# Loading the rows of w_out a pair ahead, and giving the product stage of w3 and w_out a written order on every engine

## The chip, the cores and the metric

One core of a Trainium2 chip. TensorE (PE) multiplies and loads weights, VectorE (DVE) and ScalarE (ACT) do the elementwise work, and SyncE (SP) and GpSimd (POOL) issue the DMAs here. The metric is the device time of one execution in microseconds (us). TensorE's clock has two levels, 1.2 and 2.4 GHz; the profile gives the granted clock as a share of the upper one.

## The reference

```python
scores = scale * q @ k.T - log(S)            # batch 8, 12 heads, S 448, head dim 64
attn = 1 / (1 + exp(-scores))
x = (attn @ v)  -> (3584, 768)               # tokens x model
a = x @ w1;  b = x @ w2                      # (768, 1024) each
h = a * b @ w3                               # (1024, 1024)
out = h @ w_out                              # (1024, 768)
```

The kernel takes the product of the last two matrices first: `w3 @ w_out`, 1024x768, and then `g = a * b` times that product. Every 2x2 block product is done in seven half-size products (Winograd's form), and every fp32 operand is split into a high and a low part (`high = round(x)`, `low = x - high`), so that one product becomes three matmuls: high*high, high*low, low*high.

## The kernel before

Four stages follow one another. In the first, attention runs in bursts, and beside it the weights are decoded. `up(g)` (L491) then forms `a * b` for four groups of tokens `g` and writes it to `g_dram`; the last group, `up(3)`, runs alone after the attention. It has 8 column blocks `fc` of 7 products `k` of 9 matmuls each (3 chunks `kc` by 3 parts), 63 matmuls to an `fc`. Its four banks in PSUM are `up0`, `up1` and two of `av`; product 2 goes on in the bank of product 0, 3 in that of 1, and 6 in that of 4, so product 2 may start only when ACT has copied product 0 out (`p`, L551).

While `up(3)` runs, `split_wo` (L746) prepares the operands made of `w_out`: for each of four `jc` it loads four rows from `wo_dram` (`load`, L748, on the GpSimd queue, into the pool `tw`, 7 buffers), and makes from them seven operands, each with a high part on ACT (`high_part`, L761) and a low part on DVE (`low_part`, L765). It is a generator, and one step of it follows every ten matmuls of `up(3)` (L791: a turn); between the loads of one `jc` and the first use lie two turns. At turns 40 and 41 the first two weights made of `w3` are split too (`split_w3`, L737).

Up to `order.close()` (L798) the instructions of all five engines stand in the order in which the program emits them (`manual_schedule(engines=ALL)`, L583). From L803 on only PE and SP do; for ACT, DVE and POOL the planner sets the order.

The product stage (L856 to L908) forms `w3 @ w_out`: four `ic` of seven products (counted here 0 to 27 as `n = ic * 7 + turn`, in the order of `PLAN`, L854) of 12 matmuls each. At the head of product `n` the program emits the split of the `w3` operand of product `n + 2` (`split_w3`: ACT high, DVE low, three buffers `w3s`) and the load of `n + 4` (`load_w3` on SP, two buffers `w3`, so that it waits for the low half of `n + 2`). The products of an `ic` take turns in two PSUM banks, `up` and `av` (two buffers each): turn 2 goes on in the bank that turn 0 filled, and must wait until ACT has copied turn 0 out (`p`, L881); turn 3 waits for the add of turn 1 (`u2`, L888), and so on. The results are summed and split into the seven stationary operands of the last stage (`put`, L850: high on ACT, low on DVE): A11 after turn 2, A22 after turn 4, A12 after turn 5, and S2, S3, S1, S4 after turn 6, where four sums are made first.

Then `phase_w` closes (L909), which frees the pool `p3`, and the last stage starts: product 0 has its moving block `b11` split already (in product 14 of the stage before), and the blocks `b12` and `b22` are loaded into the pool `p5`, which takes the place of `p3` (`load_block`, L820, on SP). `prepare_block(1)` splits `b21` into tiles of `p5`, too. Product 2 needs `t2 = b22 - b11`.

`combine` (L311) ends each pair of heads: ACT copies the attention result out of PSUM to `x`, and for the last quarter of the work DVE adds `x` to `s1` (L321).

Of the kernel before, what the change touches and what calls it, by code (L numbers as in the profile page):

```python
# [11 lines left out]
F32 = mybir.dt.float32  # L12
# [3 lines left out]
ALU = mybir.AluOpType  # L16
# [9 lines left out]
def sigmoid_attention_bilinear_ffn(  # L26
# [16 lines left out]
    nc = tc.nc  # L43
    B, H, D, S = qT.shape
    DM, DF = w1.shape[0], w1.shape[1] // 2
    NT = B * S
    P = 128
# [6 lines left out]
    NM = DM // 2  # L54
# [188 lines left out]
    def total(out, in0, in1, op):  # L243
        nc.vector.tensor_tensor(out=out, in0=in0, in1=in1, op=op)  # L244

    def second(g, kc):
        a11, s1 = xf.pop((g, "A11", kc)), xf[g, "A21", kc]
        total(a11, s1, a11, ALU.subtract)
        xf[g, "S2", kc] = a11
        split_operand(g, "S2", kc, a11)  # L250

    def third(g, kc):
        a22 = xf[g, "A22", kc]
        total(a22, a22, xf[g, "S2", kc], ALU.subtract)
        split_operand(g, "S3", kc, a22)

    def fourth(g, kc):
        a12 = xf.pop((g, "A12", kc))
        total(a12, a12, xf.pop((g, "S2", kc)), ALU.subtract)
        split_operand(g, "S4", kc, a12)  # L260
# [3 lines left out]
    class Units:  # L264

        def __init__(self, g):
            self.g = g
            names = ("A11", "S1", "S2") if g < NG - 1 else ("A11", "A12", "A22")
            self.left = [(name, kc) for kc in range(KH) for name in names]
            rest_of = ("A12", "A22", "S3", "S4") if g < NG - 1 else ("S2", "S3", "S1", "S4")  # L270
            self.left += [(name, kc) for name in rest_of for kc in range(KH)]
# [16 lines left out]
        def emit(self, unit):  # L288
            self.left.remove(unit)
            name, kc = unit  # L290
            if name == "S2":
                second(self.g, kc)
            elif name == "S3":
                third(self.g, kc)
            elif name == "S4":
                fourth(self.g, kc)
            else:
                split_operand(self.g, name, kc, xf[self.g, {"S1": "A21"}.get(name, name), kc])
# [12 lines left out]
    def combine(n, acc):  # L311

        b, hp = divmod(n, NPAIR)
        g, odd = divmod(b, 2)
        right, kc = divmod(hp, KH)
        name = (("A11", "A12"), ("A21", "A22"))[odd][right]
        x = xf[g, name, kc] = pf.tile([P, S], F32, name=f"{name}{kc}", bufs=1 if odd else 2)
        nc.scalar.copy(out=x, in_=acc[:, :S])
        if odd and right:
            s1 = xf[g, "A21", kc]  # L320
            total(s1, s1, x, ALU.add)  # L321

    def words(w, columns):
        return w.rearrange("(c p) (f u) -> p c f u", p=P, u=2)[:, :, columns]
# [98 lines left out]
    NH = NF // 2  # L423
    jobs = []
    for ic in range(NH):
        for i, j in ((0, 0), (0, 1), (1, 0), (1, 1)):
            src = words(w3T, slice((i * NH + ic) * P, (i * NH + ic + 1) * P))
            jobs.append((src[:, j * NH:(j + 1) * NH], None))
        for jc in (ic, ic + NH):
            for ms in (slice(0, NM), slice(NM, DM)):  # L430
                src = w_out[jc * P:(jc + 1) * P].rearrange("p (m u) -> p m u", u=2)[:, ms]
# [141 lines left out]
    def take(stream, n):  # L573
        done = 0
        for _ in itertools.islice(stream, n):
            done += 1
        return done

    ET = mybir.EngineType

    order = ExitStack()
    ALL = {ET.PE, ET.SP, ET.Activation, ET.DVE, ET.Pool}
# [143 lines left out]
    p3 = phase_w.enter_context(tc.tile_pool(name="p3", bufs=2, side="right"))  # L726
# [14 lines left out]
            w3s[n] = w  # L741

    def temp():
        return p3.tile([P, NM], F32, name="tw", bufs=7)

    def split_wo():  # L746

        def load(jc):  # L748
            rows = []
            for at in (jc, jc + NH):  # L750
                for ms in (slice(0, NM), slice(NM, DM)):
                    rows.append(temp())
                    nc.gpsimd.dma_start(out=rows[-1], in_=wo_dram[at, :, ms])
            return rows

        for jc in range(NH):
            b11, b12, b21, b22 = load(jc)
            for _ in range(2):
                yield

            def high_part(k, src):  # L761
                nc.scalar.copy(out=seven[k][0][:, jc], in_=src)
                return k, src

            def low_part(k, src):  # L765
                h, l = seven[k]
                nc.vector.tensor_tensor(out=l[:, jc], in0=src, in1=h[:, jc], op=ALU.subtract)

            last = high_part(0, b11)
            yield  # L770
            for k, src in ((1, b21), (6, b22)):
                following = high_part(k, src)
                low_part(*last)
                last = following
                yield
            t3, t2 = temp(), temp()
            for k, out, in0, in1 in (
                (3, t3, b22, b12), (4, b12, b12, b11), (2, t2, b22, b12), (5, b21, b21, t2)
            ):
                total(out, in0, in1, ALU.subtract)  # L780
                following = high_part(k, out)
                low_part(*last)
                last = following
                yield
            low_part(*last)

    pieces = split_wo()
    for n in range(2):
        load_w3(n, nc.gpsimd)
    turn = 0  # L790
    while take(filler, 10):  # L791
# [3 lines left out]
            load_w3(turn - 38, nc.gpsimd)  # L795
        turn += 1
    assert turn > 42 and not take(pieces, 1)
    order.close()  # L798
    phase_x.close()
    share_upper(None)  # L800
    phase_s.close()
    everything = ExitStack()
    everything.enter_context(tc.manual_schedule(engines={ET.PE, ET.SP}))  # L803

    ps = ctx.enter_context(tc.tile_pool(name="ps2", bufs=2, space=PSUM))
    pw = ctx.enter_context(tc.tile_pool(name="pw", bufs=4, side="left"))
    A11, A12, A22, S1, S2, S3, S4 = range(7)
# [5 lines left out]
    def stationary(which):  # L813
        return stat[which]
# [3 lines left out]
    own = {g: {} for g in range(NG)}  # L818
# [18 lines left out]
    def split_block(dst, src):  # L837
        for fs in HALVES:
            split(dst[0][:, fs], dst[1][:, fs], src[:, fs], nc.scalar.copy, nc.vector)
            yield  # L840
# [7 lines left out]
    ready_blocks = {}  # L848

    def put(which, ic, src):  # L850
        h, l = stationary(which)
        split(h[:, ic], l[:, ic], src, nc.scalar.copy, nc.vector)

    PLAN = {0: (0, True), 2: (1, True), 1: (0, False), 3: (1, False),  # L854
            4: (0, True), 5: (1, False), 6: (0, False)}
    for ic in range(NH):  # L856
        bank = {}
        for turn, (k, (which, start)) in enumerate(PLAN.items()):
            n = ic * 7 + turn
            split_w3(n + 2)  # L860
            load_w3(n + 4)
            if n in (7, 8):
                load_block(0, BLOCKS[n - 7])
            elif n == 14:
                ready_blocks[0] = moving(p4)
                for _ in split_block(ready_blocks[0], own[0]["b11"]):
                    pass
            if start:
                bank[which] = ps.tile([P, 512], F32, name="up", tag=("up", "av")[which], bufs=2)
            acc = bank[which][:, :NM]  # L870
            w = w3s.pop(n)
            th, tl = seven[k]
            for jc in range(NH):
                for m, (i, t) in enumerate(((0, th), (0, tl), (1, th))):
                    nc.tensor.matmul(  # L875
                        acc, w[:, i, jc], t[:, jc], start=start and jc == 0 and m == 0,
                        stop=jc == NH - 1 and m == 2, skip_group_check=True,
                    )
            if k == 0:
                p = temp()  # L880
                nc.scalar.copy(out=p, in_=acc)  # L881
            elif k == 1:
                c11 = temp()
                nc.scalar.copy(out=c11, in_=acc)
                put(A11, ic, acc)
            elif k == 2:
                u2 = temp()
                total(u2, acc, p, ALU.add)  # L888
            elif k == 3:
                u3 = temp()  # L890
                total(u3, acc, p, ALU.add)
            elif k == 4:
                total(u3, acc, u3, ALU.add)
                put(A22, ic, u3)
            elif k == 5:
                total(p, acc, p, ALU.add)
                put(A12, ic, p)
            else:
                total(u2, acc, u2, ALU.add)
                s3 = temp()  # L900
                total(s3, c11, u2, ALU.subtract)
                total(u2, u2, u3, ALU.add)
                total(c11, u2, c11, ALU.subtract)
                put(S2, ic, c11)
                put(S3, ic, s3)
                put(S1, ic, u2)
                total(p, p, c11, ALU.subtract)
                put(S4, ic, p)  # L908
    phase_w.close()  # L909
    p5 = ctx.enter_context(tc.tile_pool(name="p5", bufs=1, side="right"))  # L910
    for name in ("b12", "b22"):
# [65 lines left out]
    for n in range(7 * NG):  # L977
        which, bank, start = ORDER[n % 7]
# [3 lines left out]
        for mc in range(MC):  # L982
# [3 lines left out]
            acc = accs[bank, mc][:, :S]  # L986
# [38 lines left out]
```

## Time and profile before

| | us |
|---|---|
| median of 3 runs | 984.55 |
| the three runs | 983.85, 984.55, 986.32 |
| the profiled execution, its own time | 986.56 |
| its span, first to last instruction | 984.8 |
| `up(3)`, fc 1 to 7 | 607.11 to 706.90 |
| product stage of w3 and w_out | 707.98 to 773.25 |
| last stage | from 773.25 |

The trace is that of one execution, and its durations belong to it; it lies 2.0 us over the median of the runs. Times of the trace are counted from the span's start.

### The profile page before, as it was taken

The numbers are of one execution on the slowest core, as the hardware profiler recorded it, in microseconds if no ns is written. First come the engines' busy times: TensorE is split into PE (matmuls) and PEld (weight loads), VectorE is DVE, ScalarE is ACT, GpSimd is POOL, SyncE is SP. The second block draws the span as 40 slices with busy tenths as digits, with TensorE's granted clock in tenths as the row PEclk, the third lists the DMA queues.
The fourth block names the chain that finished last, engine by engine and source line by source line (L and its number), as shares of the span: only waits on it lengthen the run. The fifth ranks groups of instructions, "written<-read, shape, count | busy, mean of one in ns | idle before, by whom it ended". The sixth has DMA issues, their size and how long they took to land.

```text
span 984.8 us, 14267 instructions
## 1 busy us (share of the span) xinstructions
PE 959.2 (97%) x5190; PEld 750.4 (76%) x5190; DVE 700.3 (71%) x1154; ACT 413.5 (42%) x620; POOL 115.8 (12%) x204
## 2 busy tenths in 40 slices
PE   8999999999999999999999998799999999999998
PEld 4444666667665999849999556798889989999997
DVE  5869878987558877798868966456568777474643
ACT  6887556655556111281112660223145433223230
POOL 1110222232100121200211201211100000000000
PEclk9999999999999999999999999899999999999999
DMA  8764577776565899968999825788553334342402
GB/s 264 247 209 136 196 248 259 238 264 215 199 208 179 284 403 338 354 206 287 330 397 335 277 63 167 248 274 282 161 174 110 123 103 141 113 150 103 159 29 84
DMA packets 97605, 210.66 MB, mean 214 GB/s; under 512 B 10496, under 2 KB 57600, under 8 KB 97536
## 3 DMA queue, kind: packets, MB, share of 16 engines
q1 hardware_dynamic: 80880, 145.55, 45.0%
q0 software_dynamic: 16512, 63.98, 18.3%
q8 instruction: 41, 0.67, 0.3%
q14 instruction: 28, 0.23, 0.1%
q10 hardware_dynamic: 144, 0.23, 0.1%
HBM read 151.52 MB, written 58.20 MB: 213 GB/s over the span
## 4 chain that ended last, share of the span: by engine, by line
PE 82%; DVE 8%; DMA 5%; issue 3%; ACT 1%; POOL 1%; SPq 0%; ACTq 0%; POOLq 0%; DVEq 0%
PE up L542 36%; PE up L990 20%; PE av L219 10%; PE sp L196 7%; PE up L875 4%; PE av L227 2%; PE third L196 1%; PE sp L206 1%; DMA tw<-wo_dram 1%; DMA w<-w_dram 1%; DVE A L244 1%; DVE lS L81 1%; DMA vv<-vL 1%; DMA g_dram<-c 1%; DMA gf_b<-g_dram 1%
## 5 line engine op out<-in xcount | busy, mean ns | idle before, releaser
L542 PE MATMUL up<-hS,w 128*128 128x448 f32 x702 | 218.6, 371 | 9.7 <-DVE c L512 6.6
L542 PE MATMUL up<-hA,w 128*128 128x448 f32 x522 | 164.2, 369 | 0.4 <-ACT a L178 0.3
L542 PEld LDWEIGHTS up<-hS,w 128*128 128x128 f32 x702 | 133.5, 190 | 27.7 <-DVE c L512 7.9
L178 ACT ACTIVATE a<-sp,bias 128x896 f32<-128x896 f32 x132 | 130.0, 1011 | 52.7 <-PE sp L196 27.2
L542 PE MATMUL up<-lS,w 128*128 128x448 f32 x351 | 129.9, 370 | 0.8 <-DVE lS L81 0.8
L990 PE MATMUL up<-gl,sh 128*128 128x448 f32 x336 | 123.3, 367 | 1.5 <-DVE gl L81 1.5
L219 PE MATMUL av<-a,vv 128*64 128x448 f32 x576 | 123.7, 551 | 0.5 <-DMA vv<-vL 0.5
L990 PE MATMUL up<-gh,sh 128*128 128x448 f32 x336 | 123.3, 367 | 0.0
L990 PE MATMUL up<-gh,sl 128*128 128x448 f32 x336 | 123.3, 367 | 0.0
L542 PEld LDWEIGHTS up<-hA,w 128*128 128x128 f32 x522 | 98.7, 189 | 14.0 <-issue 4.2
L542 PE MATMUL up<-lA,w 128*128 128x448 f32 x261 | 95.8, 367 | 0.0
L551 ACT COPY p<-up 128x448 f32<-128x448 f32 x32 | 17.1, 533 | 175.9 <-PE up L542 158.8
L219 PEld LDWEIGHTS av<-a,vv 128*64 128x64 f32 x576 | 35.1, 136 | 65.9 <-issue 64.8
L512 DVE TENSOR_TENSOR u<-up,p 128x448 f32<-128x448 f32 x64 | 39.9, 623 | 58.7 <-PE up L542 55.4
L542 PEld LDWEIGHTS up<-lS,w 128*128 128x128 f32 x351 | 66.8, 190 | 7.2 <-DVE lS L81 2.1
L990 PEld LDWEIGHTS up<-gl,sh 128*128 128x128 f32 x336 | 63.1, 188 | 7.4 <-DVE gl L81 1.8
L990 PEld LDWEIGHTS up<-gh,sh 128*128 128x128 f32 x336 | 63.1, 188 | 5.8 <-ACT p L959 0.2
L990 PEld LDWEIGHTS up<-gh,sl 128*128 128x128 f32 x336 | 63.1, 188 | 5.7
L875 PE MATMUL up<-th,w3s 128*128 128x384 f32 x224 | 59.5, 344 | 4.7 <-DVE tw L244 2.0
L512 DVE TENSOR_TENSOR u<-up,u 128x448 f32<-128x448 f32 x64 | 39.8, 621 | 28.1 <-PE up L542 27.6
L80 ACT CAST gh<-gf_b 128x896 fp32r<-128x896 f32 x40 | 35.8, 941 | 56.4 <-PE up L990 55.0
L81 DVE TENSOR_TENSOR gl<-gf_b,gh 128x896 fp32r<-128x896 f32 x40 | 41.8, 1087 | 22.5 <-ACT gh L80 22.5
(107 smaller groups left out, 1556.2 us busy)
## 6 DMA issues: line engine op xcount, KB each, us to landing
w<-w_dram SPq DMA_DIRECT2D x168, 384.0 KB, 5.2
gf_b<-g_dram SPq DMA_DIRECT2D x16, 896.0 KB, 5.0
w_dram<-w POOLq DMA_DIRECT2D x36, 384.0 KB, 4.9
raw<-w POOLq DMA_DIRECT2D x16, 768.0 KB, 6.4
qk<-qT SPq DMA_DIRECT2D x48, 224.0 KB, 4.7
out<-o_sb SPq DMA_DIRECT2D x48, 224.0 KB, 1.9
qk<-kT SPq DMA_DIRECT2D x47, 224.0 KB, 5.4
vv<-vL SPq DMA_DIRECT2D x24, 384.0 KB, 4.0
```

The source lines that it names most:

```text
L80: hi_engine(out=dst_hi, in_=src)
L81: lo_engine.tensor_tensor(out=dst_lo, in0=src, in1=dst_hi, op=ALU.subtract)
L178: nc.scalar.activation(dst, src, AF.Sigmoid, bias=bias[:n], scale=scale)
L196: nc.tensor.matmul(sp[:, j], k[rows, 1, at:at + P], q[rows, 0], start=m == 0, stop=m == 2)
L206: nc.tensor.matmul(sp[HEADS[u], j], qk[rows, 1, FULL:], qk[rows, 0], start=True, stop=True)
L219: nc.tensor.matmul(acc[cols, :S], vv[:, c, at:at + D], a[:, j], start=u == 0 and c == 0, stop=u == 1 and c == NC - 2,)
L227: nc.tensor.matmul(acc[cols, :S], vs[HEADS[u], cols], a[HEADS[u], j], start=u == 1, stop=u == 0)
L512: nc.vector.tensor_tensor(out=out, in0=a, in1=b, op=ALU.add)
L542: nc.tensor.matmul(a, w[:, i, kc], x, start=bool(start) and kc == 0 and m == 0, stop=bool(stop) and kc == KH - 1 and m == 2, skip_group_ch ...
L551: nc.scalar.copy(out=p, in_=a)
L875: nc.tensor.matmul(acc, w[:, i, jc], t[:, jc], start=start and jc == 0 and m == 0, stop=jc == NH - 1 and m == 2, skip_group_check=True,)
L990: nc.tensor.matmul(acc, w[:, fc, ms], g[:, fc], start=start and fc == 0 and m == 0, stop=fc == NH - 1 and m == 2, skip_group_check=True,)
```

## The change

One line of `combine` reads the attention result from PSUM instead of ACT's copy. The rows of `w_out` get a pool of their own of eight buffers, `tw` has six instead of seven; the rows of `jc + 1` are loaded at the start of `jc`, and the first use comes four turns after the first load. A `jc` takes eight turns instead of nine. The product stage stands in program order on all five engines; `everything` (PE and SP alone) begins after it. Splits and sums of the results are put into lists: `put_later` emits the high part at once and keeps the low part for the next call; each call of `later` emits one kept low part and then one entry of the list. `later` is called once after each product, twice after turn 0, three times after turn 6. A11 is split from the copy `c11` instead of from PSUM. The two halves of block `b11` are split in products 15 and 17 instead of 14.

```diff
-            total(s1, s1, x, ALU.add)
+            total(s1, s1, acc[:, :S], ALU.add)
...
-        return p3.tile([P, NM], F32, name="tw", bufs=7)
+        return p3.tile([P, NM], F32, name="tw", bufs=6)
+
+    phase_r = ExitStack()
+    pr = phase_r.enter_context(tc.tile_pool(name="pr", bufs=8, side="right"))
...
-                    rows.append(temp())
+                    rows.append(pr.tile([P, NM], F32, name="row"))
...
+        following_rows = load(0)
+        for _ in range(4):
+            yield
         for jc in range(NH):
-            b11, b12, b21, b22 = load(jc)
-            for _ in range(2):
-                yield
+            b11, b12, b21, b22 = following_rows
+            following_rows = load(jc + 1) if jc + 1 < NH else None
...
             low_part(*last)
+            yield
...
     order.close()
+    order = ExitStack()
+    order.enter_context(tc.manual_schedule(engines=ALL))
...
-    everything = ExitStack()
-    everything.enter_context(tc.manual_schedule(engines={ET.PE, ET.SP}))
...
+    lows = []
+
+    def low_part():
+        if lows:
+            out, src, high = lows.pop(0)
+            nc.vector.tensor_tensor(out=out, in0=src, in1=high, op=ALU.subtract)
+
+    def put_later(which, ic, src):
+
+        h, l = stationary(which)
+        nc.scalar.copy(out=h[:, ic], in_=src)
+        lows.append((l[:, ic], src, h[:, ic]))
...
+        def __call__(self):
+            low_part()
+            if self.left:
+                self.left.pop(0)()
...
+        def emit():
+            total(out, in0, in1, op)
+            put_later(which, ic, out)
...
-                for _ in split_block(ready_blocks[0], own[0]["b11"]):
-                    pass
+                block = split_block(ready_blocks[0], own[0]["b11"])
+            elif n in (15, 17):
+                take(block, 1)
...
-                put(A11, ic, acc)
+                split_later(A11, ic, c11)
...
-                put(A22, ic, u3)
+                split_later(A22, ic, u3)
...
-                put(A12, ic, p)
+                split_later(A12, ic, p)
...
-                total(s3, c11, u2, ALU.subtract)
-                total(u2, u2, u3, ALU.add)
-                total(c11, u2, c11, ALU.subtract)
-                put(S2, ic, c11)
-                put(S3, ic, s3)
-                put(S1, ic, u2)
-                total(p, p, c11, ALU.subtract)
-                put(S4, ic, p)
+                sum_later(S3, ic, s3, c11, u2, ALU.subtract)
+                sum_later(S1, ic, u2, u2, u3, ALU.add)
+                sum_later(S2, ic, c11, u2, c11, ALU.subtract)
+                sum_later(S4, ic, p, p, c11, ALU.subtract)
+            for _ in range({0: 2, 6: 3}.get(turn, 1)):
+                later()
+    while later.left or lows:
+        later()
+    order.close()
+    everything = ExitStack()
+    everything.enter_context(tc.manual_schedule(engines={ET.PE, ET.SP}))
     phase_w.close()
```

## Rows read from the trace of the kernel before

**Rows 1.** The busy time of the engines in the page's first part: busy us, share of the span, instructions.

```profile
PE 959.2 (97%) x5190; PEld 750.4 (76%) x5190; DVE 700.3 (71%) x1154; ACT 413.5 (42%) x620; POOL 115.8 (12%) x204
```

**Rows 2.** Busy time by stretch (a table of windows): the stretch and its length, then for each engine its busy us and its instructions, the granted TensorE clock as a share of 2.4 GHz, the DMA engines' busy share, GB/s. The first is fc 1 to 7 of the last group of `up`, the second the product stage with `w3` and `w_out`, the third the last stage; the other two are the first microseconds after the two longest pauses of TensorE.

```profile
607.11:706.90 99.79, 93.20 (x442) 84.67 (x440) 53.02 (x97) 22.59 (x45) 18.94 (x35) 0.97 0.79 251
...
707.98:773.25 65.27, 61.63 (x337) 59.83 (x338) 45.90 (x83) 30.97 (x59) 0.87 (x2) 0.97 0.43 131
...
790.00:980.00 190.00, 190.00 (x930) 174.47 (x931) 114.44 (x137) 52.80 (x68) 0.00 (x0) 1.00 0.33 112
...
623.56:629.59 6.03, 6.03 (x17) 5.37 (x17) 4.88 (x10) 1.85 (x4) 1.11 (x3) 0.51 0.34 107
...
731.25:735.30 4.05, 4.05 (x14) 4.05 (x15) 2.95 (x5) 2.40 (x3) 0.00 (x0) 0.58 0.99 346
```

**Rows 3.** TensorE's timeline, rows from 620 to 790 us: start, duration, line, operation, out<-in, how many; in brackets the idle time just before and what ended it. The third and fourth row are three matmuls apart in the order.

```profile
623.56 0.74 PE L542 MATMUL up<-hS,w 128*128 128x448 f32 x1 [5.13 <-DVE c L512]
...
666.27 0.47 PE L542 MATMUL up<-hS,w 128*128 128x448 f32 x1 [1.46 <-DVE c L512]
...
707.98 0.41 PE L875 MATMUL up<-th,w3s 128*128 128x384 f32 x1 [1.08 <-issue]
...
720.37 0.51 PE L875 MATMUL up<-th,w3s 128*128 128x384 f32 x2
...
720.89 0.51 PE L875 MATMUL up<-th,w3s 128*128 128x384 f32 x2
...
731.25 0.41 PE L875 MATMUL up<-th,w3s 128*128 128x384 f32 x1 [2.00 <-DVE tw L244]
...
789.85 0.47 PE L990 MATMUL up<-gl,sh 128*128 128x448 f32 x1 [1.52 <-DVE gl L81]
```

**Rows 4.** The timeline of the GpSimd queue (POOL), from 609 to 618 us, columns as in group 3.

```profile
614.26 1.09 POOL L735 DMA_DIRECT2D w<-w_dram  x2 [4.39 <-DMA w<-w_dram]
615.35 2.15 POOL L753 DMA_DIRECT2D tw<-wo_dram  x4
```

**Rows 5.** ScalarE's timeline (ACT) in the same stretch, columns as in group 3.

```profile
621.87 0.51 ACT L762 CAST th<-tw 128x384 fp32r<-128x384 f32 x1 [8.40 <-DMA w<-w_dram]
623.39 0.51 ACT L762 CAST th<-tw 128x384 fp32r<-128x384 f32 x1 [1.01 <-DMA tw<-wo_dram]
624.25 0.52 ACT L762 CAST th<-tw 128x384 fp32r<-128x384 f32 x1 [0.35 <-DMA tw<-wo_dram]
```

**Rows 6.** VectorE's timeline (DVE) in the same stretch.

```profile
622.41 0.56 DVE L767 TENSOR_TENSOR tl<-tw,th 128x384 fp32r<-128x384 f32 x1 [7.04 <-DMA tw<-wo_dram]
622.89 0.62 DVE L512 TENSOR_TENSOR c<-up,u 128x448 f32<-128x448 f32 x1
```

**Rows 7.** The groups of instructions between 690 and 790 us, different shapes kept apart: line, engine, operation, out<-in, shape, how many | busy us in all, mean ns of one | idle time of the engine before them and what ended it.

```profile
L81 DVE TENSOR_TENSOR w3s<-w,w3s 128x512 fp32r<-128x512 f32 x28 | 19.3, 689 | 12.4 <-ACT w3s L80 12.3
L80 ACT CAST w3s<-w 128x512 fp32r<-128x512 f32 x28 | 17.3, 622 | 23.6 <-DMA w<-w_dram 22.2 <-issue 1.1 <-PE up L875 0.3
L81 DVE TENSOR_TENSOR sl<-tw,sh 128x384 fp32r<-128x384 f32 x24 | 13.2, 554 | 0.7 <-ACT sh L80 0.6
L80 ACT CAST sh<-tw 128x384 fp32r<-128x384 f32 x24 | 12.2, 513 | 8.8 <-DVE tw L244 8.6
L244 DVE TENSOR_TENSOR tw<-up,tw 128x384 f32<-128x384 f32 x20 | 11.1, 555 | 5.6 <-PE up L875 5.6
...
L244 DVE TENSOR_TENSOR tw<-tw 128x384 f32<-128x384 f32 x17 | 9.4, 553 | 0.1
...
L881 ACT COPY tw<-up 128x384 f32<-128x384 f32 x4 | 1.9, 474 | 4.9 <-PE up L875 4.9
```

**Rows 8.** VectorE's timeline, two low halves of `w3` products (number 11 and number 20 of 28).

```profile
731.01 0.68 DVE L81 TENSOR_TENSOR w3s<-w,w3s 128x512 fp32r<-128x512 f32 x1
...
754.99 0.69 DVE L81 TENSOR_TENSOR w3s<-w,w3s 128x512 fp32r<-128x512 f32 x1 [0.90 <-ACT w3s L80]
```

**Rows 9.** ScalarE's timeline, the high halves of the `w3` products that were loaded into the buffers which the rows of group 8 set free (number 13 and number 22).

```profile
738.21 0.62 ACT L80 CAST w3s<-w 128x512 fp32r<-128x512 f32 x1 [3.09 <-DMA w<-w_dram]
...
758.54 0.63 ACT L80 CAST w3s<-w 128x512 fp32r<-128x512 f32 x1 [1.14 <-DMA w<-w_dram]
```

**Rows 10.** VectorE's timeline at the end of the product stage and the start of the last stage.

```profile
773.29 0.56 DVE L244 TENSOR_TENSOR tw<-up,tw 128x384 f32<-128x384 f32 x1 [0.39 <-PE up L875]
...
776.90 1.22 DVE L81 TENSOR_TENSOR sl<-tw,sh 128x384 fp32r<-128x384 f32 x2
...
788.71 2.09 DVE L81 TENSOR_TENSOR gl<-t,gh 128x896 fp32r<-128x896 f32 x2
```

**Rows 11.** The timeline of the SyncE queue (SP) there.

```profile
778.19 0.92 SPq L825 DMA_DIRECT2D gf_b<-g_dram  x2
```

**Rows 12.** ScalarE's timeline there.

```profile
778.21 1.78 ACT L80 CAST gh<-gf_b 128x896 fp32r<-128x896 f32 x2 [0.68 <-PE up L990]
```

**Rows 13.** ScalarE's timeline at the end of the attention.

```profile
579.56 0.53 ACT L318 COPY A<-av 128x448 f32<-128x448 f32 x1
580.13 0.57 ACT L80 CAST hA<-A 128x448 fp32r<-128x448 f32 x1
```

**Rows 14.** VectorE's timeline there.

```profile
580.13 0.63 DVE L244 TENSOR_TENSOR A<-A,A 128x448 f32<-128x448 f32 x1 [6.09 <-ACT A L318]
580.73 0.62 DVE L81 TENSOR_TENSOR lA<-A,hA 128x448 fp32r<-128x448 f32 x1
```

More of the change, by code (lines that the diff above doesn't have):

```diff
@@ L797, in sigmoid_attention_bilinear_ffn @@
     assert turn > 42 and not take(pieces, 1)
+    phase_r.close()
     order.close()
+    order = ExitStack()
+    order.enter_context(tc.manual_schedule(engines=ALL))
     phase_x.close()
@@ L852, in put, with __init__, add_later, split_later @@
         split(h[:, ic], l[:, ic], src, nc.scalar.copy, nc.vector)
+    lows = []
[7 more added lines that the diff above has]
+        lows.append((l[:, ic], src, h[:, ic]))
+    class Later:
+        def __init__(self):
+            self.left = []
+        def __call__(self):
+            low_part()
+            if self.left:
+                self.left.pop(0)()
+    later = Later()
+    def add_later(out, in0, in1, op):
+        later.left.append(lambda: total(out, in0, in1, op))
+    def split_later(which, ic, src):
+        later.left.append(lambda: put_later(which, ic, src))
+    def sum_later(which, ic, out, in0, in1, op):
+        def emit():
+            total(out, in0, in1, op)
+            put_later(which, ic, out)
+        later.left.append(emit)
     PLAN = {0: (0, True), 2: (1, True), 1: (0, False), 3: (1, False),
```

## The prediction

> **What bounds the kernel now.** I read the busy shares first: TensorE is busy for 97% of the span, the next engine for 71% [rows 1]. So TensorE sets the time, and only its pauses and the stretches at the lower clock can change it; the number of matmuls doesn't change here. The table of windows says where they lie [rows 2]: the last stage runs 190.00 us without a pause, 930 matmuls in 190 us, 0.204 us each. `up(3)` (fc 1 to 7) is busy for 93.20 of 99.79 us at a mean clock of 0.97, the product stage for 61.63 of 65.27. TensorE's timeline then names the pauses and what ended each [rows 3]: 5.13 and 1.46 us in `up(3)`, both for an add on VectorE; 1.08 at the entry of the product stage; 2.00 in it; 1.52 in the last stage. After the 5.13 us the granted clock is 0.51 for 6.03 us, after the 2.00 us it is 0.58 for 4.05 us (the lower level, 1.2 GHz, for most of both) [rows 2]: 6.03 * 0.49 = 3.0 and 4.05 * 0.42 = 1.7 us more. The product stage has 336 matmuls; three take 0.52 us [rows 3], so its floor is 58.2 us, and it loses 7.1.
>
> **The change part by part. Rows of w_out.** The pauses of `up(3)` come about so: VectorE's queue holds `low_part` of the first row ahead of the add that empties a bank. The rows are issued at 615.35, after a wait of 4.39 us that ended at 614.26 [rows 4]; ScalarE takes the first at 621.87, the third at 623.39, the fourth at 624.25 [rows 5]; VectorE sat idle for 7.04 us until 622.41 and did the add at 622.89 [rows 6]. Before: 5.13 + 1.46 + 3.0 = 9.5 us.
> The rows of `jc` 1 to 3 are issued eight turns ahead afterwards, 80 matmuls or 16.3 us, against 6.5 to 7.3 us from issue to use here (615.35 to 621.87; the fourth is issued 3 * 0.54 = 1.6 us later [rows 4] and used at 624.25): they wait for nothing. The first `jc` can't be issued earlier, since what held GpSimd until 614.26 stays; it is only used two turns (4.1 us) later. The adds that wait now then stand ahead of `low_part`. But the third and fourth high parts come ahead of ScalarE's copy `p` of the next fc: 624.25, plus 0.52, plus 0.53 for a copy of 128x448 [rows 13], 625.3. TensorE needs that bank three products after 618.3 (9 matmuls, 1.84 us each): 623.8. So 1.5 us stay, and the gain is 9.5 - 1.5 = 8.0, between 6 (the wait grows past 2 us and the clock falls again) and 9.5. The bytes stay; DMA engines are busy for 0.79 in this stretch [rows 2], so the weights of `up` have room.
> The Trainium skill, "DMA: Bandwidth & Descriptors", section "Anatomy of one DMA — SWDGE (gpsimd) path", gives a transfer issued from GpSimd 2.0 us plus its bytes over 436e3 per us, 2.5 us for 192 KB. By that the four rows would land by 619.5, the 1.5 us would not stay, and the sum below would be 1.5 us lower. The trace disagrees: 6.5 to 7.3 us.
>
> **Entry.** The last add of `up(3)`, for which the first product waits, stands behind the low half of product 2's weights, 0.69 us [rows 7]; in the written order that comes later. Of the 1.08 us I take off 0.3 (0 to 0.7).
>
> **Product stage in program order.** Here ScalarE and VectorE must now take things as they are emitted, and I add up the order with the durations of [rows 7], 0.04 us for a handover between engines, 0.08 less from start to start of two operations in a row. At the end of an `ic` (product 6 over at T) VectorE adds (0.56), does the low half of A12, and then three calls of `later` follow: sum 0.55 on VectorE, high 0.51 on ScalarE, low 0.55 on VectorE, and only then the next sum, because a call emits the kept low part first. Each is a round trip of 1.6 us. The highs of S3, S1, S2 end at T + 2.1, 3.7 and 5.3; the add itself starts 0.4 late, behind the low half of product 8's weights, so all this is 0.4 later. Behind these highs ScalarE has the high half of product 9's weights (0.62) and only then the copy `p` of product 7 (0.47): over at T + 6.6. TensorE has done products 7 and 8 at T + 4.2 and needs that bank: a wait of 2.5 us. The add `u2` of product 8 comes behind S4's round trip and product 10's weights, over at T + 9.6: product 10 waits 1.5 more. In the trace of before the planner let the next sum go ahead of the low part before it, and the copy was in time.
> Going on so through the 28 products needs the loads. One takes 2.9 us from the low half that frees its buffer to the next high (755.68 to 758.54), and 6.5 where it is queued behind block `b21` (731.69 to 738.21) [rows 8, 9]. In the written order the low half of n + 2 stands ahead of the add of product n, so a late load holds up the adds as well. The sum gives waits of 4.0 at the first end of an `ic`, 2.9 at product 13 (its late weights ahead of an add), 6.6 at the second end (the loads are late by then, and halves of `b11`, 0.9 us on ScalarE and 1.05 on VectorE each [rows 12, 10], are in the queues), 4.8 at the third: 18.3 us. 58.2 + 18.3 = 76.5, with 0.5 for the lower clock 77.0. The same addition over the order that the trace shows gives 64.0, where the stage took 65.3, so I trust it to some 2 us. 77.0 - 65.3 = 11.7 lost. Without the late load behind `b21`, and with no waits that grow from `ic` to `ic`, it is 58.2 + 3 * 4.0 = 70.2, 4.9 lost; with the clock falling after each wait, 14.
>
> **Release of p3.** The last stage's loads wait for the last low part of the product stage: TensorE is through at 773.25, VectorE's last low ends at 776.90 + 1.22 = 778.12 [rows 10], SP issues `b12` and `b22` at 778.19 [rows 11], ScalarE starts on `b21` at 778.21 [rows 12], and the low half of `t2` at 788.71 ends the pause before 789.85 [rows 10, 3]. So 4.9 us after the last product now. Afterwards four round trips stand there: 0.04 + 0.47 + 0.47 + 4 * 1.61 = 7.4, and 7.5 with the last handover. 2.6 lost, as all of it is one chain; 1.6 if the planner puts the low half of `t2` a step earlier, 4.5 if the clock falls in the two pauses (1.7 each as above, one of them covered).
>
> **The add from PSUM.** `combine`'s add can start without ScalarE's copy (579.56), but the operation after it on VectorE starts at 580.73, when the high part that ScalarE took from 580.13 to 580.70 is there [rows 13, 14]; that stays. 0, and the work that hides it is that cast. The bank stays taken until VectorE comes by: up to 1 us lost; up to 0.3 won, where VectorE is free at once. The eight buffers cost nothing: their first use waits for the same 614.26.
>
> **Sum.** -8.0 - 0.3 + 11.7 + 2.6 + 0 = +6.0. The profiled execution would go from 986.56 to 992.6; it lies 2.0 above the median, so from 984.55 I get 990.5 us.
>
> **Rivals.** *The written order is cheap (faster).* The mechanism is the one point T + 4.2: if the copy `p` is over by then, because the round trips of a call overlap more than I add up (2.4 us less over three), no wait stands at the ends of an `ic`. The stage then keeps its 65.3 or comes down towards 61: -8.3 + 2.6 = -5.7 to -10, 979 to 974.5. For it: VectorE is busy for only 45.90 of 65.27 us [rows 2], there is room to spread. Against it: each high needs its sum, each low its high, and the order leaves nothing in between. *The waits don't grow.* 4.9 instead of 11.7: -0.8, 983.8, no change. For it: the addition ignores that a waiting TensorE lets the loads catch up before the next end. Against it: the block halves and `b21` fall into the second `ic`. *The rows are late all the same*, because GpSimd's queue holds each load behind stores of `g` that wait for VectorE: half of the 8.0 gone, 994.5. Against it: eight turns hold one fc, and a store waits for one add and one product.
>
> **How the numbers follow.** The forecast, slower by 3 to 10 us, 0.52; late rows on top 0.08; waits that don't grow 0.17; cheap order 0.23. Differences under 0.3% (3 us) can't be told from none. So faster 0.23, same 0.17, slower 0.60. Around the likeliest alone 987 to 995; for 8 in 10 I reach down into the cheap order, 978, and up to 996 (bounds 14 and 4.5 together give 998).
>
> **What would show it.** No idle of 5 us in `up(3)`, one of about 1.5 near 624. In the product stage TensorE's idle time ended by ScalarE's `tw` copy (L881's successor) at turn 2 of `ic` 1 to 3, 2 us or more each, and then by VectorE's add at turn 3. VectorE waiting for `sh` on ScalarE some 16 times, half a microsecond each. The SP load of `b12` 7.5 us after the last product. The prediction is wrong if the copy `p` follows its product at once; then the forecast's 11.7 are gone, and the kernel is faster.

## The result and the profile after

The median of six runs is 991.74 us (989.78 to 994.98), against 984.3 for the kernel before (983.85 to 987.3): a ratio of 1.007, 95% interval 1.0049 to 1.0092. The change makes the kernel slower by 7.4 us; forecast were 6.2 us more (990.5). The profiled execution is the slowest of the six, 994.98 us with a span of 993.2, so its stages add up to 8.4 us, not to 7.4; its stage lengths are those of one execution, 3.2 us above the median, and differences of a microsecond or two against another profile are not to be leaned on.

The engines' line of the page: TensorE has 5.8 us more busy time than in [rows 1] for the same matmuls, as its granted clock was lower (0.988 in the mean, 0.993 before).

```profile
PE 965.0 (97%) x5190; PEld 756.0 (76%) x5190; DVE 700.8 (71%) x1154; ACT 413.7 (42%) x620; POOL 115.3 (12%) x204
```

The table of windows, one stretch for each stage (length; busy us and instructions of PE, PEld, DVE, ACT, POOL; granted clock; DMA share; GB/s). `up(3)` with the entry takes 116.26 us, where it went from 584.08 to 707.98 before, 123.9. The product stage takes 78.01 instead of the 65.1 to the first matmul of the last stage (773.09), at a mean clock of 0.89 instead of 0.97 [rows 2]. The last stage takes 214.16 instead of 211.7. With 0.7 us by which `up(3)` began later: 0.7 - 7.6 + 12.9 + 2.4 = 8.4. The 7.6 is the upper end of what the profiles show: with the new loads and four turns, `up(3)` with the entry takes 116.26 to 119.01 us in this profile and those of five of the runs below; with the old loads 122.71 to 123.90 in three.

```profile
584.77:701.03 116.26, 109.34 (x516) 95.99 (x517) 73.12 (x135) 26.30 (x54) 19.18 (x36) 0.99 0.74 236
701.03:779.04 78.01, 67.15 (x337) 64.85 (x337) 46.24 (x82) 31.61 (x59) 0.88 (x2) 0.89 0.37 109
779.04:993.20 214.16, 208.24 (x1009) 190.14 (x1008) 128.69 (x156) 61.93 (x82) 0.00 (x0) 0.99 0.33 112
```

TensorE's timeline, the pauses that stand in the place of [rows 3]. Those of 5.13 and 1.46 us in `up(3)` are gone, and one of 2.02 came, for ScalarE's copy `p`. In the product stage the three long ones (2.66, 3.01, 3.53) are all ended by ScalarE's copy of turn 0 (L928, L881 before), at turn 2 of `ic` 1, 2 and 3; behind two of them stands one for VectorE's add (0.55, 0.96). All the pauses of the stage come to 10.7 us.

```profile
625.14 0.74 PE L542 MATMUL up<-hA,w 128*128 128x448 f32 x1 [2.02 <-ACT p L551]
...
701.03 0.41 PE L922 MATMUL up<-th,w3s 128*128 128x384 f32 x1 [1.14 <-issue]
...
722.66 0.44 PE L922 MATMUL up<-th,w3s 128*128 128x384 f32 x1 [2.66 <-ACT tw L928]
...
726.29 0.66 PE L922 MATMUL up<-th,w3s 128*128 128x384 f32 x1 [0.55 <-DVE tw L244]
...
744.16 0.44 PE L922 MATMUL up<-th,w3s 128*128 128x384 f32 x1 [3.01 <-ACT tw L928]
...
749.03 0.41 PE L922 MATMUL up<-th,w3s 128*128 128x384 f32 x1 [0.96 <-DVE tw L244]
...
765.71 0.69 PE L922 MATMUL up<-th,w3s 128*128 128x384 f32 x1 [3.53 <-ACT tw L928]
...
789.03 0.74 PE L1040 MATMUL up<-gh,sh 128*128 128x448 f32 x1 [2.40 <-ACT p L1009]
```

How such a wait comes about is read from the two queues side by side. VectorE around the end of the first `ic` (product 6 ends at about 715.8, two products of 2.08 us before the idle time that begins at 722.66 - 2.66): the add at 716.48, then for each of S3, S1 and S2 a sum (L244), a pause of 0.58 for ScalarE, a low part (L866).

```profile
716.48 0.55 DVE L244 TENSOR_TENSOR tw<-up,tw 128x384 f32<-128x384 f32 x1
716.94 0.55 DVE L866 TENSOR_TENSOR sl<-tw,sh 128x384 fp32r<-128x384 f32 x1
717.41 0.55 DVE L244 TENSOR_TENSOR tw<-tw 128x384 f32<-128x384 f32 x1
718.54 0.56 DVE L866 TENSOR_TENSOR sl<-tw,sh 128x384 fp32r<-128x384 f32 x1 [0.58 <-ACT sh L871]
719.01 0.55 DVE L244 TENSOR_TENSOR tw<-tw 128x384 f32<-128x384 f32 x1
720.14 0.56 DVE L866 TENSOR_TENSOR sl<-tw,sh 128x384 fp32r<-128x384 f32 x1 [0.58 <-ACT sh L871]
720.62 0.55 DVE L244 TENSOR_TENSOR tw<-tw 128x384 f32<-128x384 f32 x1
722.26 0.69 DVE L81 TENSOR_TENSOR w3s<-w,w3s 128x512 fp32r<-128x512 f32 x1 [1.10 <-ACT w3s L80]
```

ScalarE in the same stretch: three high parts, each 1.09 us of waiting after the last, then the high half of product 9's weights, and only then the copy `p` of product 7, from 722.14 to 722.61. TensorE goes on at 722.66.

```profile
717.99 0.51 ACT L871 CAST sh<-tw 128x384 fp32r<-128x384 f32 x1 [2.16 <-DVE tw L244]
719.60 0.51 ACT L871 CAST sh<-tw 128x384 fp32r<-128x384 f32 x1 [1.09 <-DVE tw L244]
721.20 0.51 ACT L871 CAST sh<-tw 128x384 fp32r<-128x384 f32 x1 [1.09 <-DVE tw L244]
721.62 0.61 ACT L80 CAST w3s<-w 128x512 fp32r<-128x512 f32 x1
722.14 0.47 ACT L928 COPY tw<-up 128x384 f32<-128x384 f32 x1
```

The end of the stage, VectorE and then the SyncE queue. The last product ends at 779.20 (its last matmul starts at 778.86 and takes 0.34); the last low part ends at 786.68, 7.5 us later (4.9 in [rows 10]), and the loads of `b12` and `b22` go out at 786.76.

```profile
779.24 0.56 DVE L244 TENSOR_TENSOR tw<-up,tw 128x384 f32<-128x384 f32 x1 [1.06 <-PE up L922]
...
786.12 0.56 DVE L866 TENSOR_TENSOR sl<-tw,sh 128x384 fp32r<-128x384 f32 x1 [0.58 <-ACT sh L871]
...
797.15 2.09 DVE L81 TENSOR_TENSOR gl<-t,gh 128x896 fp32r<-128x896 f32 x2
```

```profile
786.76 0.92 SPq L832 DMA_DIRECT2D gf_b<-g_dram  x2
```

### The profile page after: what moved, and what is told of

Read it like the earlier page. It is cut to its first block, busy times and chain, and to the rows that moved or that the text cites. A ratio compares the mean times of both kernels' runs of the same rounds, so it can differ in the third digit from the quotient of the medians.

```text
span 993.2 us, 14264 instructions
## 1 busy us (share of the span) xinstructions
PE 965.0 (97%) x5190; PEld 756.0 (76%) x5190; DVE 700.8 (71%) x1154; ACT 413.7 (42%) x620; POOL 115.3 (12%) x204
## 4 chain that ended last, share of the span: by engine, by line
PE 83%; DVE 8%; DMA 4%; ACT 3%; issue 2%; POOL 1%; ACTq 0%; DVEq 0%; POOLq 0%
PE up L542 38%; PE up L1040 20%; PE av L219 10%; PE sp L196 7%; PE up L922 2%; PE av L227 2%; PE third L196 2%; PE sp L206 2%; DMA w<-w_dram 2%; DVE tw L244 1%; DVE A L244 1%; ACT w3s L80 1%; DVE w3s L81 1%; DVE lS L81 1%; DMA row<-wo_dram 1%
## 5 line engine op out<-in xcount | busy, mean ns | idle before, releaser
L542 PE MATMUL up<-hS,w 128*128 128x448 f32 x702 | 216.1, 367 | 3.0 <-DVE hS L80 2.3
L1040 PE MATMUL up<-gl,sh 128*128 128x448 f32 x336 | 123.9, 369 | 0.0
L922 PE MATMUL up<-th,w3s 128*128 128x384 f32 x224 | 64.2, 364 | 12.0 <-ACT tw L928 9.2
```

The costliest lines, as they stand in the source:

```text
L542: nc.tensor.matmul(a, w[:, i, kc], x, start=bool(start) and kc == 0 and m == 0, stop=bool(stop) and kc == KH - 1 and m == 2, skip_group_ch ...
L922: nc.tensor.matmul(acc, w[:, i, jc], t[:, jc], start=start and jc == 0 and m == 0, stop=jc == NH - 1 and m == 2, skip_group_check=True,)
L1040: nc.tensor.matmul(acc, w[:, fc, ms], g[:, fc], start=start and fc == 0 and m == 0, stop=fc == NH - 1 and m == 2, skip_group_check=True,)
```

## The experiments

Each is given with its edit against the kernel named; the median of the kernel before on the same chips was 984.4 to 984.5. Stage lengths run from the first matmul of a stage to the first of the next.

**The rows alone.** The kernel before with the part on `w_out`:

```diff
-        return p3.tile([P, NM], F32, name="tw", bufs=7)
+        return p3.tile([P, NM], F32, name="tw", bufs=6)
+    pr = phase_r.enter_context(tc.tile_pool(name="pr", bufs=8, side="right"))
...
+        following_rows = load(0)
+        for _ in range(4):
+            yield
         for jc in range(NH):
-            b11, b12, b21, b22 = load(jc)
-            for _ in range(2):
-                yield
+            b11, b12, b21, b22 = following_rows
+            following_rows = load(jc + 1) if jc + 1 < NH else None
...
             low_part(*last)
+            yield
```

> The kernel before with the part on w_out alone: eight buffers, a pair ahead, four turns before the first use; the product stage as it was. Theory (the written order of the product stage is what costs, the rows are a gain of their own): up(3) with the entry keeps the 7.6 us that it won, the product stage stays at 65 us, the time is 976.5 (974 to 979). Rival (the gain in up(3) is only lent, and comes back as waits in the product stage, whatever its order): 981 to 985.

977.85 us, ratio 0.993 (0.9913 to 0.9946). The product stage in its table of windows:

```profile
703.24:768.20 64.96, 60.21 (x336) 57.97 (x337) 45.64 (x83) 30.84 (x59) 0.87 (x2) 1.00 0.42 131
```

64.96 us, as before. So the rows are a gain of 6.6 us of their own by the medians, and nothing of it comes back in the product stage. The expected 7.6 us of `up(3)` with the entry are not in this profile: it takes 119.01 us (584.23 to 703.24), 4.9 less than before. Its pause of 2.05 us at 626.02 is that of the changed kernel, but TensorE is busy for 2.8 us more, at a mean clock of 0.97 instead of 0.99; the profiled execution is 3.8 us above the median.

**The product stage alone.** The kernel before with all of the change from `order.close()` on; `split_wo`, `tw` and `combine` as they were:

```diff
     order.close()
+    order = ExitStack()
+    order.enter_context(tc.manual_schedule(engines=ALL))
...
-                put(A11, ic, acc)
+                split_later(A11, ic, c11)
...
-                put(S2, ic, c11)
+                sum_later(S3, ic, s3, c11, u2, ALU.subtract)
...
+            for _ in range({0: 2, 6: 3}.get(turn, 1)):
+                later()
```

> The kernel before with the product stage of the change alone; rows of w_out loaded as before. Theory: product stage +12.9 us and the release of p3 +2.5, with nothing won: 999.5 (996 to 1002). Rival (the gain of up(3) is lent): up(3) is late and the stage pays less, 992 or less.

1000.49 us, ratio 1.0162 (1.0147 to 1.0177). The stage:

```profile
707.90:785.10 77.20, 63.22 (x336) 60.32 (x337) 46.00 (x82) 31.60 (x59) 0.87 (x2) 0.96 0.35 110
```

77.20 us, and 214.2 behind it. The stage alone costs 16.1 us by the medians, the rows alone win 6.6; together that is +9.5, and 7.4 were measured. The 2.1 us between them are no more than the medians leave open (about 2 us on either side for the changed kernel, 1.5 for each of the two runs).

**The next sum ahead of the kept low part.**

```diff
         def __call__(self):
-            low_part()
+            kept = len(lows)
             if self.left:
                 self.left.pop(0)()
+            if kept:
+                low_part()
```

> The changed kernel; a call of later emits the next sum and its high part first and the kept low part behind them. Order still written on all engines. Theory (three round trips of 1.6 us hold ScalarE's copy p): a call takes VectorE 1.0 instead of 1.6 us, the wait at turn 2 falls from 2.7 to 3.5 us to under 1.5, the product stage from 78 to some 72 us, the last low part comes 5.1 instead of 7.5 us after the last product: 984 (981 to 988). Rival (what costs is what is queued, the block halves in products 15 and 17 and the splits beside the adds, not the order within a call): 990 to 992.

984.26 us, ratio 1.0011 (0.999 to 1.0032): 7.5 us off the changed kernel for the order of two statements. The profile is that of an execution of 989.2 us. VectorE at the end of the first `ic`: after the add at 718.66 sum, low, sum, low stand 0.47 us apart, without a pause; in the changed kernel a sum and its low part took 1.6.

```profile
718.66 0.55 DVE L244 TENSOR_TENSOR tw<-up,tw 128x384 f32<-128x384 f32 x1
719.25 0.56 DVE L244 TENSOR_TENSOR tw<-tw 128x384 f32<-128x384 f32 x1
719.73 0.55 DVE L866 TENSOR_TENSOR sl<-tw,sh 128x384 fp32r<-128x384 f32 x1
720.19 0.55 DVE L244 TENSOR_TENSOR tw<-tw 128x384 f32<-128x384 f32 x1
720.66 0.55 DVE L866 TENSOR_TENSOR sl<-tw,sh 128x384 fp32r<-128x384 f32 x1
```

TensorE's waits at turn 2 fall to 0.84, 1.37 and 0.77 us, as expected (under 1.5). The product stage takes 72.2 us (703.38 to 775.6), the last stage 211.8, as before the change; the last low part ends 5.1 us after the last product. So the second term of the loss, the late release, goes with the first. The longest pauses left in the stage are 2.37 us at product 12 and 2.04 at turn 3 of the third `ic`, both for an add.

**The planner's order for the same lists.**

```diff
-    order = ExitStack()
-    order.enter_context(tc.manual_schedule(engines=ALL))
+    everything = ExitStack()
+    everything.enter_context(tc.manual_schedule(engines={ET.PE, ET.SP}))
     phase_x.close()
...
     while later.left or lows:
         later()
-    order.close()
-    everything = ExitStack()
-    everything.enter_context(tc.manual_schedule(engines={ET.PE, ET.SP}))
```

> The changed kernel with all its lists, calls and moved halves, but in the product stage only TensorE and SyncE in written order; the planner places ScalarE and VectorE. Theory: the written order is the whole loss, so 977 (974 to 980), within 2 us of the rows alone. Rival (the spreading itself costs): 988 to 992.

975.28 us, ratio 0.991 (0.9881 to 0.9939). The stage, and ScalarE at the end of its first `ic`: the copy `p` (L928) comes straight after the first high part, at 722.26.

```profile
705.03:766.20 61.17, 60.12 (x336) 58.06 (x337) 46.20 (x83) 31.10 (x59) 0.87 (x2) 1.00 0.45 138
```

```profile
721.84 0.52 ACT L871 CAST sh<-tw 128x384 fp32r<-128x384 f32 x1 [1.23 <-DVE tw L244]
722.26 0.47 ACT L928 COPY tw<-up 128x384 f32<-128x384 f32 x1
```

61.17 us: shorter than the 65.1 of the kernel before, and near the floor of 58.2. So this written order is the whole loss: without it the kernel is 16.5 us faster by the medians. The rest of the edit in the stage (the lists, the halves of `b11` moved, A11 from `c11`; not tried one by one), with the planner placing it, wins some 4 us of the stage. By the medians it is 2.6 us (975.28 against 977.85 for the rows alone) with intervals that overlap, so it is the stage's length that shows it: 61.17 here and 60.98 in the run with six turns, against 65.1 and 64.96 without the lists.

**TensorE kept at work through the waits.**

```diff
             acc = bank[which][:, :NM]
+            if turn == 2 and ic > 0:
+                idle = ps.tile([P, 512], F32, name="sp", tag="sp", bufs=2)
+                for _ in range(14):
+                    nc.tensor.matmul(
+                        idle[:, :NM], seven[0][0][:, 0, :P], seven[0][0][:, 1], start=True, stop=True
+                    )
             w = w3s.pop(n)
```

> The changed kernel with 14 extra matmuls of 128x384 (2.4 us, results not used) ahead of turn 2 of ic 1 to 3, so that TensorE works through the three long waits (2.66, 3.01, 3.53 us) and its clock has no cause to fall. Theory (the dates at which ScalarE's copy p and VectorE's add u2 come are set by those two engines; the lower clock after a wait mostly runs down inside the next wait): the waits that are left sit at turn 3, the product stage loses 1 to 3 us of its 78, the time is 989.5 (988 to 991). Rival (the lower clock adds up: mean clock 0.89 over 78 us is 8.6 us of its own): 984 or less.

993.83 us (993.38 to 994.28), a ratio of 1.0097 to the kernel before (1.0078 to 1.0117). The stage, and TensorE's pauses at the first end of an `ic` and after it:

```profile
700.10:777.53 77.43, 69.33 (x379) 66.77 (x379) 46.08 (x82) 31.46 (x59) 0.88 (x2) 0.98 0.35 109
```

```profile
721.70 0.44 PE L928 MATMUL up<-th,w3s 128*128 128x384 f32 x1 [0.21 <-ACT tw L934]
...
725.34 0.41 PE L928 MATMUL up<-th,w3s 128*128 128x384 f32 x1 [1.25 <-DVE tw L244]
...
730.81 0.41 PE L928 MATMUL up<-th,w3s 128*128 128x384 f32 x1 [1.04 <-DVE tw L244]
...
733.85 0.41 PE L928 MATMUL up<-th,w3s 128*128 128x384 f32 x1 [0.72 <-DVE tw L244]
```

The clock stays at 0.98, and the stage is hardly shorter, 77.43 us against 78.01. The wait at turn 2 shrinks to 0.21, but from there to where TensorE goes on at turn 3 it is 3.64 us (721.70, 725.34), and in the changed kernel 3.63 (722.66, 726.29); products 12 and 13 wait for adds which they didn't have to wait for at the lower clock. Waits (77.43 - 69.33 = 8.1 us) and extra matmuls (3 times 2.4) take 15.4 us together, where the changed kernel is without work for 78.01 - 67.15 = 10.9; the other matmuls are busy for 62.0 us instead of 67.2. So the lower clock costs next to nothing of its own here: most of it runs down inside the next wait. Where no wait follows, it does cost: from the third turn 2 to the end of the stage it is 12.1 us here and 13.3 in the changed kernel. Half of this gain had been lost before (that turn 2 comes 65.36 us after the stage began, 64.68 in the changed kernel); why, is open.

The last stage shows the same exchange: it takes 214.17 us, as in the changed kernel (214.16), with a pause of 2.40 at its product 1 as there, but with the clock at 1.00 behind it, and then with a second one, for the low half of `t2`, that the changed kernel doesn't have:

```profile
796.80 0.47 PE L1046 MATMUL up<-gl,sh 128*128 128x448 f32 x1 [1.41 <-DVE gl L81]
```

The time missed both statements: it is 2.1 us above the changed kernel's median, where 1 to 3 less were expected. The profiles don't hold that difference (this span is 991.7 us, that of the changed kernel 993.2, in the slowest of its six runs, which spread over 5.2 us); its source stays open. That the clock adds up, 984 or less, is ruled out.

**One more round trip ahead of the copy.**

```diff
-            for _ in range({0: 2, 6: 3}.get(turn, 1)):
+            for _ in range({6: 4}.get(turn, 1)):
```

> The changed kernel with four calls of later after turn 6 and one after turn 0, instead of three and two: one more round trip of 1.6 us in front of ScalarE's copy p. Theory: each of the three waits at turn 2 grows by about 1.6 us and the wait at turn 3 shrinks, the addition of the order gives the stage 4 us more: 995.7 (993.5 to 998), the release of p3 as in the changed kernel. Rival (the copy p waits for something else, a load of w3 or TensorE's own lateness): 990 to 992.5.

997.12 us, ratio 1.013 (1.0113 to 1.0147). TensorE's waits at turn 2:

```profile
724.59 0.44 PE L922 MATMUL up<-th,w3s 128*128 128x384 f32 x1 [4.18 <-ACT tw L928]
...
747.69 0.69 PE L922 MATMUL up<-th,w3s 128*128 128x384 f32 x1 [5.14 <-ACT tw L928]
...
769.22 0.44 PE L922 MATMUL up<-th,w3s 128*128 128x384 f32 x1 [4.41 <-ACT tw L928]
```

4.18, 5.14 and 4.41 us against 2.66, 3.01 and 3.53: 1.5, 2.1 and 0.9 more, 1.5 in the mean for a round trip of 1.6. So the copy waits for the round trips, and a wait at turn 3 is not left at any of the three ends. The stage takes 79.7 us in this profile, 1.7 more than in the changed kernel's, where 4 were expected; by the medians the kernel is 5.4 us slower than the changed one.

**Planner, and six turns before the first use.** As the run with the planner, and:

```diff
-        for _ in range(4):
+        for _ in range(6):
             yield
```

> The planner's order in the product stage, all else as changed, and six turns instead of four between the first load of w_out and its first use. Theory: the pause of 2.0 us that the change left in up(3), for ScalarE's copy behind two high parts, goes where it stands; in the planner run with four turns it did not stand, as up(3) came later there. 974 (972 to 976.5). Rival (six turns push the last splits of w_out onto the entry of the product stage): 977 or more.

974.44 us, ratio 0.9893 (0.9868 to 0.9917), the fastest version of the study: 17.3 us below the changed kernel and 10.0 below the one before. Its product stage takes 61.0 us and `up(3)` has no pause from 620 us to its end. What the six turns add to the planner's 975.28 is within the spread of both; the pause of 2.02 us stood in neither profile, so that it goes with six turns is not shown.

**The add ahead of the copy.** The kernel before with

```diff
-        nc.scalar.copy(out=x, in_=acc[:, :S])
         if odd and right:
             s1 = xf[g, "A21", kc]
-            total(s1, s1, x, ALU.add)
+            total(s1, s1, acc[:, :S], ALU.add)
+        nc.scalar.copy(out=x, in_=acc[:, :S])
```

> The kernel before with the add of combine reading PSUM, and emitted ahead of ScalarE's copy of the same bank. Theory (two engines that read one bank are put one behind the other, in the order of emission): at the end of the attention the add starts some 2.5 us earlier and ScalarE's copy of that pair waits for it or follows it; no change of the time, 984 (982 to 988). Rival (the add waits for something else that came late): it starts after ScalarE's copy as before.

988.98 us in the one run, 4.5 above the median of before. At the end of the attention the add now comes first, and ScalarE's copies wait for it, 2.60 and 4.18 us (ScalarE's timeline):

```profile
590.09 0.53 ACT L321 COPY A<-av 128x448 f32<-128x448 f32 x1 [2.60 <-DVE A L244]
...
596.76 0.53 ACT L321 COPY A<-av 128x448 f32<-128x448 f32 x1 [4.18 <-DVE A L244]
```

VectorE in turn waits 1.20 and 1.50 us for the high part that ScalarE makes behind each of these copies (`hA`, for the low part `lA`), and its own high part `hS`, which TensorE needs, stands behind that. TensorE has a pause of 4.39 us where 1.72 stood:

```profile
599.87 0.74 PE L542 MATMUL up<-hS,w 128*128 128x448 f32 x1 [4.39 <-DVE hS L80]
```

So two readers of one bank take their turns in the order of emission, as the theory had it. The time missed the expected range (982 to 988), but what this order costs is not shown by a single run, 1.6 us above the slowest of eleven of the kernel before. In its profile `up(3)` with the entry takes 123.55 us, no more than before: the pauses of 5.13 and 1.46 us are 0.71 and 0.85 here. What is longer is the part ahead of it; `up(3)` begins at 587.55, 3.5 us later than before, and another run has it at 587.01 with the copy first.

## Why the prediction was right, point by point

**Rows of w_out.** Forecast -8.0 and -0.3 at the entry, measured -7.6 for both in the profile, -4.9 in that of the rows alone and -6.6 by that run's median. The pause that stays was the one named: ScalarE's copy `p` behind the high parts of the third and fourth row, which it takes at 623.25 and 624.15, with the copy at 624.56.

```profile
621.08 0.51 ACT L767 CAST th<-row 128x384 fp32r<-128x384 f32 x1 [8.28 <-DMA row<-wo_dram]
623.25 0.51 ACT L767 CAST th<-row 128x384 fp32r<-128x384 f32 x1 [1.66 <-DMA row<-wo_dram]
624.15 0.51 ACT L767 CAST th<-row 128x384 fp32r<-128x384 f32 x1 [0.38 <-DMA row<-wo_dram]
624.56 0.53 ACT L551 COPY p<-up 128x448 f32<-128x448 f32 x1
```

It is 2.02 us instead of 1.5, and the clock falls after it (0.71 mean from 625.14 to 631.00). The 0.3 us at the entry didn't come: 1.14 us of idle time before the first product, 1.08 in [rows 3].

**Product stage.** Forecast +11.7, measured +12.9; a round trip was taken as 1.61 us, and sums stand 1.60 and 1.61 apart on VectorE. The path is the one forecast: the copy `p` behind three round trips and product 9's weights, then the add of the product after it. The first end of an `ic`, added up to 2.5 and 1.5 us, has 2.66 and 0.55.

The sizes were only partly right. At turns 2 and 3 the addition had 4.0, 6.6 and 4.8; the trace has 3.2, 4.0 and 3.5, and no wait of 2.9 at product 13, 10.7 instead of 18.3. (A wait for an add behind late weights stands in the run with the next sum first, 2.37 us at product 12: VectorE had been idle for 4.27 us, and ScalarE had waited 3.42 for the load.) In place of the rest stands the lower clock (0.89 over 78 us; TensorE is busy for 67.2 us where the floor is 58.2), for which the addition had put in 0.5. So two terms were mis-sized in opposite directions, and that the total came out is more than luck only because they are mostly the same microseconds: with the clock up, in the run with the extra matmuls, waits and extra matmuls come to 15.4 us in a stage of 77.43.

Two smaller readings: VectorE waited for `sh` 13 times, 7.5 us in all; 16 times were named. The prediction's list of pauses of the kernel before leaves one out, 1.04 us at 747.24 for a low half of `w3s`; no term of the sum uses it.

**Release of p3.** Forecast +2.6, with the last low part at 7.5 us; measured +2.4 and 7.5. One step of the path was another. The prediction led the chain over `b21` to the low half of `t2`. In the trace what holds TensorE is the pause at product 1 of the last stage (2.40 us before 789.03), and it ends with ScalarE's copy `p` of product 0 (L1009), in whose bank product 1 goes on. Two casts of `b21` stand ahead of that copy in ScalarE's queue, and they waited until `p3` was free:

```profile
786.77 1.78 ACT L80 CAST gh<-gf_b 128x896 fp32r<-128x896 f32 x2 [0.68 <-DVE sl L866]
788.46 1.39 ACT L1009 COPY p<-up 128x448 f32<-128x448 f32 x3
```

Before, the casts began at 778.21 [rows 12] and the copies at 779.90, and TensorE had no pause there. The low half of `t2` at 797.15 is 8.4 us later than in [rows 10], and no pause is left before it: TensorE had lost 2.40 us and ran at a clock of 0.76 from 789.03 to 796.00.

**The add from PSUM.** The cost of nothing fits, but no run has this line alone: `up(3)` begins at 584.77, and over the profiles with this line at 582.45 to 587.01, at 584.08 to 585.19 in those with the old one. One step of the reason was wrong. The prediction said that the add can start without ScalarE's copy. It started at 580.81, when the copy of the same bank (580.24 to 580.77) was over. ScalarE, then VectorE:

```profile
580.24 0.53 ACT L318 COPY A<-av 128x448 f32<-128x448 f32 x1
```

```profile
580.81 0.62 DVE L244 TENSOR_TENSOR A<-A,av 128x448 f32<-128x448 f32 x1 [6.09 <-ACT A L318]
```

**Rivals.** "The written order is cheap" needed the copy to be over 4.2 us after T; it was over 6.8 us after (715.8 to 722.61). "The waits don't grow" gave the stage 4.9 more and it had 12.9; the waits at turn 2 did grow, from 2.66 to 3.01 and 3.53, but by less than the addition had. Late rows did not occur: ScalarE waited for rows three times, 10.3 us in all by the list of waits, and all three belong to `jc` 0 (before 621.08, 623.25 and 624.15 above).

## What to carry to other kernels

Writing out the order of an engine's queue fixes what stands behind each wait. When an engine hands a result to another engine and gets something back from it, put other work of its own in between, and not at once the operation that needs the answer: the order of two statements was worth 7.5 us here. Before taking an order from a planner, add up its queues at the places where results pile up, and look what the first instruction behind the pile is; here it was a copy that TensorE needed. A gain and a loss in one change hide each other: the rows won 6.6 us and the lists 2.6 to 4, and both were covered by an order that cost 16.

## What the runs showed that I had not expected

Two engines that read one PSUM bank did so one after the other, in the order of emission: with the copy first the add began 0.04 us after the copy's end (580.77, 580.81), though VectorE had been idle for 6.09 us; with the add first, ScalarE waited 2.60 and 4.18 us. Whether the program's semaphores or the bank make it so was not tried.

A clock that falls after a wait need not cost its share, as long as another wait follows in which it runs down. The product stage was 78.01 us long at 0.89 and 77.43 at 0.98; behind its last long wait, with no other to follow, it was 1.3 us shorter with the clock up.
